# Products with v of unit 1 given to the scheduler ahead of the scores of units 2 and 3

## The chip, the cores and the metric

The kernel runs on one core of one Trainium2 chip. The metric is the device time of one execution in microseconds (us), taken as the median of several runs. Engines of the core: PE (TensorE: matmuls, with PEld for its weight loads), DVE (VectorE), ACT (ScalarE), POOL (GpSimd) and SP (SyncE, which issues all the DMAs here). Each engine runs its own instructions in a fixed order, and waits on semaphores for the others.

## The reference

Softmax attention inside chunks of 64 tokens, whose result goes through a gated feed-forward layer (sigmoid gate). All matrices are fp32.

```python
q_c, k_c, v_c = (z.reshape(8, 8, 9, 64, 64) for z in (q, k, v))       # batch, heads, chunks, 64 tokens, 64
scores = np.matmul(q_c, k_c.transpose(0, 1, 2, 4, 3)) / np.sqrt(64)
scores = scores - np.max(scores, axis=-1, keepdims=True)
attn = np.exp(scores)
attn = attn / (np.sum(attn, axis=-1, keepdims=True) + 1e-09)
x = np.matmul(attn, v_c)...reshape(4608, 512)                          # tokens x (heads x 64)
gate = 1.0 / (1.0 + np.exp(-(x @ w_gate)))                             # w_gate, w_val: 512 x 1536
out = gate * (x @ w_val) @ w_out                                       # w_out: 1536 x 512
```

## The kernel before, in words

**Tiles.** The 4608 tokens are 9 blocks `m` of 512, and the hidden width of 1536 is 12 slices `f` of 128. An fp32 number is carried as two parts, high and low (fp32r), so that each product is three matmuls: high by high, high by low, low by high. The weights come in as 64-bit words; `convert_weights(f, part)` makes the two parts of one 128x512 piece (part 0 gate, 1 value, 2 outer): on ACT L129, L130 and the cast L136 for the high part, on DVE L131, L132, L134 and L137 for the low part. Each piece is loaded by `load_weights` (L108, 512 KB per DMA) into a few raw buffers, and a buffer is loaded again only when its piece is converted.

**Attention.** It is cut into 36 units `j`; four make a block: unit 4m+2h+u gives half `h` (256 tokens) of block m, and half `u` of its 512 columns. Units 0 and 1 are the first half of block 0, units 2 and 3 its second half, units 4 to 7 block 1. A unit goes through these steps:

- `load` (L149, L152: q and k) and `load_values` (L158: v), DMAs from SP;
- `scores`: 16 PE matmuls `sc` (L170) into a PSUM tile, then on DVE the row maximum `mx` (L181). Either DVE subtracts it (L190) and the exponential comes later (capital S: units 0 and 2), or ACT does subtraction, exponential and sum in 8 activations (L195; small s: units 1 and 3);
- `softmax`: for S units the exponential on ACT (L201) and its sum on DVE (L203); for all, on DVE, L206, the reciprocal L208 and the scaling L209;
- `transposes`: 4 PE transposes `tp` (L215), evicted into `pbd` by L218 and L220 (or L222);
- `values`: 16 PE matmuls `av` (L231), evicted into the feed-forward's input `xt`: high part on ACT (L249), low part on DVE (L250).

`sc`, `tp` and `av` share two PSUM buffers (`ps_a`, tag psa): the third tile of the three kinds in a row has to wait until the first is evicted. Which tile gets which buffer follows the order in which the program calls the steps.

**Feed-forward.** `step(m, f, span)` is `hidden`: 12 matmuls `g` of the gate (L261) into bank g0, the sigmoid `hf` on ACT (L270), 12 matmuls of the value into bank g1, their product on DVE (L272), and its two parts `hh` (ACT, L274) and `hl` (DVE, L276). `down` adds its product with the outer weights into `acc` (L287). In block 0, slices 0 and 1 are done by halves: "a" is the first 256 tokens (needs units 0 and 1), "b" the rest (needs units 2 and 3). The sigmoid and the exponential need different tables on ACT; a change of table is an instruction of its own (ACT_TABLE_LOAD).

**Order.** Two strings of tokens, START and MIDDLE (L29 to L38), say in which order the program calls the steps: L, V load; S, s scores; E softmax; T, t transposes; A values; W loads and C converts weights (`C1.0`: slice 1, part 0); H is `step` (`H0.1a`: block 0, slice 1, first half); D is `down`. In START this order is no execution order: a scheduler takes the calls in that order as their priority, and sets the order of each engine from it and from its own idea of what is ready. From MIDDLE on PE keeps the order of the program (L711), and in `rest` DVE too. `rest` goes on with blocks 1 and 2, while POOL makes sums of weights (`keep_sums`, L338 to L347) which go to DRAM; blocks 3 to 8 are done in pairs by a scheme with 7 products instead of 8, with those sums as operands.

**What the change touches.** The token A1, `values(1)`: the 16 `av` matmuls of unit 1, and the ACT and DVE evictions L249 and L250 behind them.

Of the kernel before, what the change touches and what calls it, by code (L numbers as in the profile page):

```python
# [26 lines left out]


START = """  # L29
L0 L1 V0 W0o S0 s1 V1 E0 W0u t0 C0.0 E1 L2 t1 L3 C0.1 A0 W1u S2 C0.2 s3 A1 C1.0 H0.0a E2 W1o E3 C1.1  # L30
T2 W2u T3 D V3 L4 V2 C2.0 A2 C1.2 A3 L5 H0.1a H0.0b W3o D W3u C2.1 C3.0 H0.1b D s4 W4u W2o H0.2 C3.2
C2.2 W4o C3.1 C4.0 D W5u E4 C4.1 C5.0 C5.1 H0.3 D s5 C4.2 t4 E5 W6u H0.4 D W7u C6.0 V5 W6o C7.0 C6.1
H0.5 D W5o L6 C5.2 L7 C6.2 H0.6 V4 W8u C7.1 D W7o C8.0 t5 C8.1 C7.2 H0.7 D W9u
# [710 lines left out]
```

## Time and profile before

| what | us |
|---|---|
| median of 3 runs | 950.69 (950.37 to 951.47) |
| the profiled execution | 949.0 |
| its span, first to last instruction | 947.2 |
| PE busy | 927.4 (98%) |
| DVE busy | 601.1 (63%) |
| ACT busy | 340.5 (36%) |
| POOL busy | 139.0 (15%) |

Times in all rows count from the start of the span. The table says how much of the whole an engine was busy; a stage can have another bound than the whole, so the rows of the section below go by stretches of time. In a timeline an instruction's line gives its start, its length and, in brackets, how long its engine had idled before it and what ended that. Lengths overlap: in a full queue the next instruction starts before the one ahead of it has ended. The profile also gives the granted clock of PE (1.00 is 2.4 GHz, 0.50 is 1.2 GHz).

### The profile page before, as it was taken

The numbers are of one execution on the slowest core, as the hardware profiler recorded it, in microseconds if no ns is written. First come the engines' busy times: TensorE is split into PE (matmuls) and PEld (weight loads), VectorE is DVE, ScalarE is ACT, GpSimd is POOL, SyncE is SP. The second block draws the span as 40 slices with busy tenths as digits, with TensorE's granted clock in tenths as the row PEclk, the third lists the DMA queues.
The fourth block names the chain that finished last, engine by engine and source line by source line (L and its number), as shares of the span: only waits on it lengthen the run. The fifth ranks groups of instructions, "written<-read, shape, count | busy, mean of one in ns | idle before, by whom it ended". The sixth has DMA issues, their size and how long they took to land.

```text
span 947.2 us, 13080 instructions
## 1 busy us (share of the span) xinstructions
PE 927.4 (98%) x4960; PEld 762.0 (80%) x4960; DVE 601.1 (63%) x999; ACT 340.5 (36%) x556; POOL 139.0 (15%) x204
## 2 busy tenths in 40 slices
PE   6999999999999999999999999999999999999998
PEld 4778888888888887888887888888878888888886
DVE  6899973576576656766766666767686334445332
ACT  6899752233233242233142522232324221121222
POOL 1000006970079880000000000000000000000000
PEclk7999999999999999999999999999999999999999
DMA  8699894442243448657675756665565565556561
GB/s 290 210 305 298 313 305 168 134 145 78 64 137 112 134 141 312 203 200 229 205 246 207 254 186 219 211 220 201 190 222 197 193 208 183 203 184 215 218 222 45
DMA packets 81279, 189.61 MB, mean 200 GB/s; under 512 B 7488, under 2 KB 38208, under 8 KB 76608
## 3 DMA queue, kind: packets, MB, share of 16 engines
q1 hardware_dynamic: 81216, 188.77, 59.5%
q8 instruction: 39, 0.64, 0.3%
q14 instruction: 24, 0.20, 0.1%
HBM read 150.99 MB, written 37.75 MB: 199 GB/s over the span
## 4 chain that ended last, share of the span: by engine, by line
PE 81%; POOL 6%; DMA 6%; ACT 3%; DVE 2%; issue 1%; SPq 1%; POOLq 0%; ACTq 0%; DVEq 0%
PE acc L496 20%; PE cy L421 16%; PE g L261 13%; PE cz L421 11%; PE cx L421 10%; PE acc L287 6%; DMA sums<-a_both 3%; PE sc L170 3%; PE av L231 3%; POOL a_both L347 2%; POOL a_sum L344 2%; POOL a_both L346 1%; POOL a_val L338 1%; DMA out<-ob 1%; DMA wr<-sums 1%
## 5 line engine op out<-in xcount | busy, mean ns | idle before, releaser
L261 PE MATMUL g<-xt,w 128*128 128x512 f32 (+1 forms) x960 | 207.5, 371 | 3.0 <-ACT xt L249 1.3
L261 PEld LDWEIGHTS g<-xt,w 128*128 128x128 f32 x960 | 168.5, 189 | 36.3 <-ACT xt L249 1.7
L496 PE MATMUL acc<-wr,hh 128*128 128x512 f32 x576 | 177.8, 390 | 0.0
L421 PE MATMUL cy<-xc,wr 128*128 128x512 f32 x648 | 159.2, 389 | 0.9 <-DVE u L439 0.9
L421 PEld LDWEIGHTS cy<-xc,wr 128*128 128x128 f32 x648 | 121.5, 188 | 26.5 <-DVE u L439 1.3
L496 PEld LDWEIGHTS acc<-wr,hh 128*128 128x128 f32 x576 | 107.9, 188 | 22.7 <-ACT raw L242 0.3
L496 PE MATMUL acc<-wr,hl 128*128 128x512 f32 x288 | 112.7, 391 | 2.7 <-DVE hl L488 2.7
L421 PE MATMUL cz<-xc,wr 128*128 128x512 f32 x432 | 106.1, 391 | 1.1 <-DMA wr<-sums 1.1
L421 PE MATMUL cx<-xc,wr 128*128 128x512 f32 x432 | 106.0, 391 | 0.0
L560 DVE STREAM_TRANSPOSE pbd<-pr 32x256 f32<-32x256 f32 x224 | 97.6, 436 | 4.0
L488 DVE TENSOR_TENSOR hl<-hid,hh 128x512 fp32r<-128x512 f32 x72 | 49.5, 688 | 78.8 <-ACT hh L486 78.5
L421 PEld LDWEIGHTS cz<-xc,wr 128*128 128x128 f32 x432 | 80.5, 188 | 19.0 <-issue 2.5
L421 PEld LDWEIGHTS cx<-xc,wr 128*128 128x128 f32 x432 | 80.6, 188 | 17.5 <-issue 1.0
L287 PE MATMUL acc<-w,hh 128*128 128x512 f32 x288 | 90.4, 395 | 1.0 <-ACT hh L274 1.0
L486 ACT CAST hh<-hid 128x512 fp32r<-128x512 f32 x72 | 44.8, 622 | 127.1 <-PE acc L496 103.7
L338 POOL TENSOR_TENSOR a_val<-w 128x256 f32<-128x256 f32 x48 | 37.3, 798 | 202.2 <-ACT xt L249 144.7
L496 PEld LDWEIGHTS acc<-wr,hl 128*128 128x128 f32 x288 | 54.0, 188 | 16.0 <-DVE hl L488 4.8
L439 DVE TENSOR_TENSOR u<-cy,s 128x512 f32<-128x512 f32 x36 | 24.8, 688 | 63.3 <-PE cy L421 61.3
L272 DVE TENSOR_TENSOR hf<-g,hf 128x512 f32<-128x512 f32 (+1 forms) x40 | 25.4, 635 | 60.6 <-PE g L261 59.6
L287 PEld LDWEIGHTS acc<-w,hh 128*128 128x128 f32 x288 | 52.7, 188 | 13.1 <-issue 1.9
L456 DVE TENSOR_TENSOR u<-cy,s 128x512 f32<-128x512 f32 x36 | 24.9, 691 | 50.7 <-PE cy L421 50.5
L287 PE MATMUL acc<-w,hl 128*128 128x512 f32 x144 | 56.1, 389 | 0.0
(103 smaller groups left out, 1009.4 us busy)
## 6 DMA issues: line engine op xcount, KB each, us to landing
wr<-sums SPq DMA_DIRECT2D x72, 512.0 KB, 4.6
wr<-outer SPq DMA_DIRECT2D x36, 1024.0 KB, 4.9
w_raw<-w_in SPq DMA_DIRECT2D x36, 512.0 KB, 5.0
wr<-given SPq DMA_DIRECT2D x36, 512.0 KB, 3.7
sums<-a_both SPq DMA_DIRECT2D x24, 512.0 KB, 3.5
qt<-q_in SPq DMA_DIRECT2D x36, 256.0 KB, 4.4
kbd<-k_in SPq DMA_DIRECT2D x72, 128.0 KB, 4.4
vt<-v_in SPq DMA_DIRECT2D x36, 256.0 KB, 4.0
```

The source lines that it names most:

```text
L170: nc.tensor.matmul(sc[c * D:(c + 1) * D, (2 * a + t) * P:(2 * a + t + 1) * P], lhsT=s["qt"][:, a, n0:n0 + D], rhs=s["kb"][:, a, :, n0:n0 + D],
L231: nc.tensor.matmul(av[a * D:(a + 1) * D, c * P:(c + 1) * P], lhsT=s["vt"][:, a, c, :], rhs=pb[:, 4 * a + c, :, :], start=True, stop=True,)
L261: nc.tensor.matmul(ps[:, tok], lhsT=wt[f, which][:, wpart, c:c + P], rhs=x[:, part, i, tok], start=n == 0, stop=n == 11)
L272: nc.vector.tensor_tensor(out=hf, in0=pv, in1=hf, op=ALU.mult)
L287: nc.tensor.matmul(acc[m, t], lhsT=hx[:, ts], rhs=wt[f, 2][:, wpart], start=f == 0 and i == 0, stop=f == NF - 1 and i == 2,)
L338: nc.gpsimd.tensor_tensor(out=val[:, 2 * n:2 * n + 2], in0=parts[:, 0], in1=parts[:, 1], op=ALU.add)
L421: nc.tensor.matmul(bank, lhsT=lhs(wpart, c), rhs=x[:, part, c], start=start and k == 0, stop=stop and k == 5, skip_group_check=True)
L456: nc.vector.tensor_tensor(out=u3, in0=y, in1=s1, op=ALU.add)
L486: nc.scalar.copy(hh, h)
L488: nc.vector.tensor_tensor(out=hl, in0=h, in1=hh.bitcast(F32), op=ALU.subtract)
L496: nc.tensor.matmul(acc[m, t], lhsT=hx[:, ts], rhs=wo[f][:, wpart], start=f == 0 and i == 0, stop=f == NF - 1 and i == 2)
L560: nc.vector.transpose(out=pb[dst, :, c, h, i, :], in_=ps[src, h::2, k, :])
```

## The change

One token moves within START, seven places forward: A1 now stands right behind A0, ahead of the raw load of slice 1 (W1u), the scores of units 2 and 3 (S2, s3) and a conversion (C0.2).

```diff
 START = """
-L0 L1 V0 W0o S0 s1 V1 E0 W0u t0 C0.0 E1 L2 t1 L3 C0.1 A0 W1u S2 C0.2 s3 A1 C1.0 H0.0a E2 W1o E3 C1.1
+L0 L1 V0 W0o S0 s1 V1 E0 W0u t0 C0.0 E1 L2 t1 L3 C0.1 A0 A1 W1u S2 C0.2 s3 C1.0 H0.0a E2 W1o E3 C1.1
```

No instruction is added by the program, but the scheduler makes another order of all engines but POOL. ACT's order before has 36 ACT_TABLE_LOADs, and the changed one 38. In the rows below, numbers behind a name tell tiles apart (tiles may have another number in the changed program); two `sc` or `av` rows "x8" with 64 partitions stand for 16 matmuls.

**PE, first half of block 0.** `sc_228` and `sc_249` before are the scores of units 2 and 3 (`sc_240` and `sc_261` in the changed program), `av_270` (`av_225`) are the values of unit 1, g0_291 and g1_306 the first products of slice 0. Before:

```order
L231 MATMUL av_213<-pbd_89,vt_122 64x128 x8
L170 MATMUL sc_228<-kbd0_87,qt_191 64x128 x8
L261 MATMUL g0_291<-xt_222,w_178 128x256
L261 MATMUL g1_306<-xt_222,w_178 128x256
L170 MATMUL sc_249<-kbd1_88,qt_202 64x128 x8
L261 MATMUL g0_291<-xt_222,w_178 128x256 x5
L261 MATMUL g1_306<-xt_222,w_178 128x256 x3
L231 MATMUL av_270<-pbd_89,vt_159 64x128 x8
```

Changed:

```order
L231 MATMUL av_213<-pbd_89,vt_122 64x128 x8
L231 MATMUL av_225<-pbd_89,vt_159 64x128 x8
L261 MATMUL g0_291<-xt_222,w_178 128x256
L170 MATMUL sc_240<-kbd0_87,qt_191 64x128 x8
L170 MATMUL sc_261<-kbd1_88,qt_202 64x128 x8
L261 MATMUL g0_291<-xt_222,w_178 128x256 x5
L261 MATMUL g0_291<-xt_234,w_178 128x256 x6
L261 MATMUL g1_306<-xt_222,w_178 128x256 x6
L261 MATMUL g1_306<-xt_234,w_178 128x256 x6
L261 MATMUL g0_421<-xt_222,w_282 128x256
```

The values of unit 1 stand ahead of both scores, and the 24 products of slice 0 follow in one piece.

**ACT, softmax of units 2 and 3.** `early` is the tile of the exponentials, L201 that of unit 2 and L195 that of unit 3; hf_304 and hh_320 belong to slice 0 of the first half, w_282 to slice 1. Before:

```order
L201 ACTIVATE early_85<-early_85 128x512
L136 CAST w_240<-w_raw_241 128x512
L249 CAST xt_279<-av_270 128x2x256
L195 ACTIVATE early_85,sums_261<-sc_249,mx_258 128x64 x8
L270 ACT_TABLE_LOAD
L270 ACTIVATE hf_304<-g0_291 128x256
L136 CAST w_282<-w_raw_283 128x512
```

Changed:

```order
L136 CAST w_252<-w_raw_253 128x512
L129 ACTIVATE w_raw_283<-w_raw_237 128x512
L270 ACT_TABLE_LOAD
L270 ACTIVATE hf_304<-g0_291 128x256
L195 ACT_TABLE_LOAD
L195 ACTIVATE early_85,sums_273<-sc_261,mx_270 128x64 x8
L136 CAST w_282<-w_raw_283 128x512
L274 CAST hh_320<-hf_304 128x256
L201 ACTIVATE early_85<-early_85 128x512
```

Both exponentials moved behind the first sigmoid, so that the table goes to the sigmoid and back, and that of unit 2 moved behind that of unit 3.

**ACT and PE, second half of block 0.** tp_344 and tp_354 are the transposes of units 2 and 3, av_386 and av_406 their values, hf_434 the sigmoid of slice 1 for the first half. ACT before:

```order
L218 COPY pbd_89<-tp_344 64x8x64
L218 COPY pbd_89<-tp_354 64x8x64
L129 ACTIVATE w_raw_378<-w_raw_351 128x512
L130 ACTIVATE w_raw_351<-w_raw_351 128x512
L129 ACTIVATE w_raw_398<-w_raw_331 128x512
L136 CAST w_282<-w_raw_283 128x512
L249 CAST xt_222<-av_386 128x2x256
L130 ACTIVATE w_raw_331<-w_raw_331 128x512
L249 CAST xt_279<-av_406 128x2x256
```

ACT changed:

```order
L218 COPY pbd_89<-tp_344 64x8x64
L218 COPY pbd_89<-tp_354 64x8x64
L130 ACTIVATE w_raw_351<-w_raw_351 128x512
L270 ACT_TABLE_LOAD
L270 ACTIVATE hf_434<-g0_421 128x256
L136 CAST w_377<-w_raw_378 128x512
L249 CAST xt_222<-av_386 128x2x256
L249 CAST xt_234<-av_406 128x2x256
```

PE before, with g0_454 and g1_469 the products of slice 0 for the second half, and sc_555 and sc_732 the scores of units 4 and 5:

```order
L261 MATMUL g0_454<-xt_222,w_178 128x256 x6
L261 MATMUL g0_454<-xt_279,w_178 128x256
L170 MATMUL sc_555<-kbd0_87,qt_371 64x128 x7
L261 MATMUL g0_454<-xt_279,w_178 128x256 x5
L170 MATMUL sc_555<-kbd0_87,qt_371 64x128
L170 MATMUL sc_732<-kbd1_88,qt_417 64x128 x7
L261 MATMUL g1_469<-xt_222,w_178 128x256 x6
```

PE changed:

```order
L261 MATMUL g0_454<-xt_222,w_178 128x256 x6
L261 MATMUL g0_454<-xt_234,w_178 128x256
L170 MATMUL sc_555<-kbd0_87,qt_371 64x128 x5
L261 MATMUL g0_454<-xt_234,w_178 128x256 x5
L261 MATMUL g1_469<-xt_222,w_178 128x256 x6
```

The transposes' evictions and the `xt` casts now have a third table load between them, and of the scores of units 4 and 5 only 10 of 32 matmuls stand ahead of g1_469, where 30 stood before; the other 22 come in pieces of 6, 10 and 6 behind later products.

## Rows read from the trace of the kernel before

**Rows 1.** The page: busy us of each engine; granted clock of 40 slices.

```profile
PE 927.4 (98%) x4960; PEld 762.0 (80%) x4960; DVE 601.1 (63%) x999; ACT 340.5 (36%) x556; POOL 139.0 (15%) x204
PEclk7999999999999999999999999999999999999999
```

**Rows 2.** Stretches: length, busy us (instructions) by engine, granted clock, DMA share, GB/s.

```profile
17.70:42.00 24.30, 20.20 (x176) 17.04 (x175) 22.10 (x44) 21.19 (x51) 0.00 (x0) 0.93 0.64 217
42.00:56.00 14.00, 13.63 (x76) 11.60 (x75) 12.17 (x27) 10.45 (x30) 0.00 (x0) 1.00 0.90 276
56.00:74.00 18.00, 18.00 (x82) 14.55 (x82) 16.87 (x32) 17.37 (x39) 0.00 (x0) 1.00 0.91 307
265.00:947.00 682.00, 673.65 (x3439) 552.90 (x3437) 411.21 (x650) 195.06 (x271) 80.54 (x112) 1.00 0.58 196
```

**Rows 3.** Timeline of PE: start, length, what, idle time before it and releaser.

```profile
16.34 1.39 PE L170 MATMUL sc<-kbd,qt 128*64 128x128 f32 x16
...
20.39 1.98 PE L170 MATMUL sc<-kbd,qt 128*64 128x128 f32 x16
...
26.63 1.45 PE L261 MATMUL g<-xt,w 128*128 128x256 f32 x10 [0.23 <-DVE xt L250]
29.56 1.23 PE L215 MATMUL tp<-ident,early 128*128 128x128 f32 x8 [1.48 <-DVE early L209]
...
33.91 1.97 PE L231 MATMUL av<-pbd,vt 128*64 128x128 f32 x32
35.81 2.65 PE L261 MATMUL g<-xt,w 128*128 128x256 f32 x20
...
41.28 1.70 PE L261 MATMUL g<-xt,w 128*128 128x256 f32 x12
...
55.80 5.73 PE L261 MATMUL g<-xt,w 128*128 128x512 f32 x24 [0.37 <-ACT hf L270]
...
73.24 5.60 PE L261 MATMUL g<-xt,w 128*128 128x512 f32 x24
```

**Rows 4.** Stretches as in rows 2, short ones, for PE's clock.

```profile
10.00:12.00 2.00, 0.49 (x3) 0.52 (x4) 1.26 (x4) 2.00 (x16) 0.00 (x0) 0.54 1.01 410
...
22.00:23.00 1.00, 1.00 (x7) 0.70 (x4) 0.95 (x2) 1.00 (x2) 0.00 (x0) 0.50 1.00 401
...
28.00:30.00 2.00, 0.52 (x5) 0.42 (x4) 2.00 (x8) 1.97 (x5) 0.00 (x0) 1.00 0.49 139
```

**Rows 5.** Timeline of DVE.

```profile
19.29 0.69 DVE L250 TENSOR_TENSOR xt<-av,xt 128x512 fp32r<-128x512 f32 x1
...
28.72 1.29 DVE L209 TENSOR_TENSOR early<-early,inv 128x512 f32<-128x512 f32 x2
...
38.44 0.69 DVE L250 TENSOR_TENSOR xt<-av,xt 128x512 fp32r<-128x512 f32 x1
```

**Rows 6.** Timeline of ACT.

```profile
19.93 0.66 ACT L129 ACTIVATE w_raw<-w_raw 128x512 f32<-128x512 f32 x1
20.49 0.66 ACT L130 ACTIVATE w_raw<-w_raw 128x512 uint32<-128x512 uint32 x1
21.81 0.63 ACT L201 ACTIVATE early<-early 128x512 f32<-128x512 f32 x1 [0.66 <-DVE early L190]
...
25.75 0.32 ACT L195 ACTIVATE early<-sc,mx 128x64 f32<-128x64 f32 x1
...
28.25 1.28 ACT L270 ACT_TABLE_LOAD   x1
29.54 0.38 ACT L270 ACTIVATE hf<-g 128x256 f32<-128x256 f32 x1
```

**Rows 7.** Issues by line in the first 80 us: KB each, median us to landing.

```profile
w_raw<-w_in SPq DMA_DIRECT2D x24, 512.0 KB, 5.4
```

**Rows 8.** Waits after 330 us: engine line, for whom, us in total, times, longest.

```profile
PE cz L421 <- DMA wr<-sums: 1.1, 1, 1.1
```

**Rows 9.** Timeline of POOL: the start of its second run of sums.

```profile
265.13 1.94 POOL L338 TENSOR_TENSOR a_val<-w 128x256 f32<-128x256 f32 x2 [55.94 <-DMA out<-ob]
```

## Prediction

> **What bounds the kernel now.** I read the page first: PE is busy for 927.4 of the span of 947.2 us, and its clock is below full only at the very start [rows 1]. So the end moves by what PE loses or wins: idle time, and time at half clock. The stretches then show where the change can reach. From 17.7 to 42 PE is busy for 20.20 of 24.30 us, with DVE at 22.10 and ACT at 21.19; from 42 to 56 it idles 0.37 us, and from 56 to 74 not at all [rows 2]. The loss lies ahead of 42, where the softmax of units 2 and 3 has to get through ACT and DVE, both full. Behind 42, what PE has lost comes back only if it idles less later, and up to 56 there is 0.37 us to be had.
>
> **The change, part by part.** I walk through the new order with the durations of the old one.
>
> *Scores.* The `av` of unit 1 takes the place of the first `sc`, at 16.34 [rows 3]; what it reads is evicted there, since the old `sc` waited for the same buffer. The first `sc` (unit 2) now needs the buffer of unit 0's `av`, and DVE frees that at 19.29 + 0.69 = 19.98 [rows 5]. So it starts at 20.0, not 16.34, and unit 3's `sc` follows it, not ahead of 21.6. PE's clock was down to 0.54 and 0.50 after it had idled, in 10 to 12 and in 22 to 23, and the 16 `sc` matmuls then took 1.98 [rows 3, 4]. PE is as idle in 17 to 20 as before, so I take half speed here too: the two end at 23.6. Before, the second ended at 22.4. At full clock it would be about 22.2, which is the low end of this step: 1.4 sooner for PE, and 0.6 for ACT, whose casts wait for loads and DVE work too.
>
> *First products.* The other 23 `g` matmuls follow in one piece at 0.13 each (20 in 2.65 [rows 3]): done at 26.7. Before, they ended at 26.63 + 1.45 = 28.1 [rows 3]. That is the good side of the change, 1.4 us.
>
> *Softmax of units 2 and 3.* Now the bad side. DVE reduces unit 2's scores at 21.7 and only then finishes the weights that ACT casts at 23.0. With 0.56 from one ACT operation to the next (19.93 to 20.49 [rows 6]) the sigmoid's table load starts at 24.2. From there, by the rows: load 1.28, sigmoid 0.38, second load 1.28, and 2.5 for the 8 activations of unit 3 (25.75 to 28.25) [rows 6]: 29.65. Only then come the cast of slice 1's gate weights (to 30.25), `hh`, and the exponential of unit 2 (to 31.1; before, it began at 21.81 [rows 6]). PE needs that cast: it idles from 26.7 to 30.3, some 3.5 us, where its longest gap was 1.48 [rows 3]. DVE goes on with unit 2's sum at 31.2, a weight operation of the queue, two reciprocals, and the two L209 at 33.2 to 34.5. Before they ran from 28.72 to 30.01 [rows 5], so they are 4.5 us late. After its gap PE has 11 matmuls to do, `acc` and `g`, ahead of the transposes. After a gap of 1.48 the clock stayed at 1.00 [rows 4]; after one of 3.5 I expect half clock, and the 11 then last to about 34.3. That hides behind the late L209, so the clock costs little.
>
> *Second half.* The transposes run at 34.3 to 35.5, and ACT evicts them, but then reloads the sigmoid's table (36.6 to 37.9) and does a sigmoid and a weight cast ahead of the two L249 (38.7 and 39.2). DVE's second L250 ends at 41.3; before, at 38.44 + 0.69 = 39.1 [rows 5]. The last 5 matmuls of g0_454 wait for it, and g1_469 begins at 42.3, where it stood at 41.28 [rows 3]: **1.0 us**. Ahead of it stand 10 matmuls of the next scores, before 30. The other 20 have to be done later, on a PE with no idle time: at 0.062 each (32 of the same form in 1.97 [rows 3]) that is **1.2 us**.
>
> *Loads, and SP's queue.* `vt` of unit 2 no longer waits for unit 1's `av`, and the weights of slice 3 are asked for about 1.3 us sooner, since the buffer that they take is converted sooner. I count nothing for it: PE doesn't idle behind 42 for want of them.
>
> *ACT from 44 to 58.* PE would reach block 0's slice 3 at 57.5 (42.3, the 14.15 us from 41.28 to the gap ahead of 55.80, and 1.0 for 16 of the scores still owed). It needs the sigmoid of slice 2, which was 0.37 late [rows 3]. In the new order the slice 4 weights stand ahead of it, asked for at about 44.3; with 5.4 to landing [rows 7] they come at 49.7. Then 6 operations at 0.56, a load, 8 activations of unit 4, a load and the sigmoid: 58.5. If the load hides altogether, waits on DVE still make it 58.0. So PE idles 0.5 to 1.0, where it was 0.37: 0.1 to 0.7 more, **0.5** taken.
>
> *ACT from 58 to 76.* Between the sigmoids of slices 3 and 5 the new order has 23 plain ACT operations, the activations of unit 5 and two table loads: 23 x 0.56 + 2.5 + 2 x 1.28 = 17.9. PE needs 73.24 - 55.80 = 17.4 [rows 3] and 4 more matmuls: 17.7. A wait of 0.2, or 1 if a weight load is late: **0.3**. Behind that ACT has no more work left than before, while PE comes later.
>
> Sum: 1.0 + 1.2 + 0.5 + 0.3 = **3.0 us**. The lower bound is 1.9 (clock at full in the first step, and no wait at 58 and 76), the upper 4.5 (half clock until the `av` of units 2 and 3, 1 us more, and late weights). The profiled execution took 949.0, so it would take 952.0; the median lies 1.7 above that execution, and I add the 3.0 to it: **953.7**. All that follows is released by PE: even POOL's second run, at 265.13, waits for an output that PE's `acc` lets go [rows 9].
>
> On the table loads: a load and the first activation behind it follow at once, 28.25 to 29.54 [rows 6]. The Trainium skill (ScalarE: Activation LUTs, "What ACT_TABLE_LOAD costs") adds a drain to each switch and puts it at about 2.66 us. The row shows no such drain. By the skill's figure the two extra loads would cost up to 2.8 us more than I have, an estimate of 955 to 956; by the row they don't. The same page's rule for kernel authors, to do all of one table set before switching, speaks against this order, and there the rows agree.
>
> **The rivals.** I call a change of over 0.2% (1.9 us) one that a measurement can tell from none.
>
> *Not slower: the two added table loads hide.* Place: ACT, 24 to 38. The first would hide if ACT reached it while it waits for g0 (done at 25.2); the third, if it is through before the `av` of unit 2. Price: 2 x 1.28 = 2.6 off the start of g1_469, now 39.7; with the 1.2 of scores owed, and no late sigmoid at 56, that is -0.4 to -0.7, some 950.2. It decides from the point where DVE's L209 start before 31. For it: I know ACT's waits only to half a microsecond. Against it: ACT is at 21.19 of 24.30 [rows 2], and what stands ahead of each load is ready.
>
> *Given back later.* PE idles 8.35 us behind 265 [rows 2]. Where it waits for something that runs by another clock, as for the sums from DRAM (1.1 us, once [rows 8]), a later PE waits less. With the 0.37 as well that leaves +1.5: 952.2. Against it: the sums come from POOL, which starts on an output of PE's [rows 9].
>
> *Weights late.* ACT is at 17.37 of 18 us from 56 to 74, DVE at 16.87 [rows 2]. Two loads more are 2.6 us of ACT; if none of that finds a gap and the conversions fall behind PE, it comes on top: +5.6, 956.3. Against it: PE is 3 us later too, and ACT idled 3.55 of 14 us from 42 to 56 [rows 2].
>
> *Faster by over 0.2%.* The one piece of products (1.4) would have to count in full with nothing late behind it, and the softmax chain not to count at all: 948.5.
>
> **How the numbers follow.** Forecast (+1.9 to +4.5, likeliest 3.0) 0.53; weights late 0.12; given back 0.18; loads hidden 0.12; faster 0.05. Slower is 0.53 + 0.12 = 0.65, the same 0.18 + 0.12 = 0.30, faster 0.05. The range takes in the forecast, the late weights and most of what is given back: 951.6 to 956.3. It leaves out the hidden loads and the faster case, 0.17, and a little beyond.
>
> **What would show it.** PE's gap of about 3.5 us ending at 30.3, and half clock behind it; L209 at 33 to 34.5; the L249 of units 2 and 3 behind a table load, near 39; g1_469 at 42.3 and `sc` in pieces behind it; the start of PE's slice 3 at about 58, and POOL's second run at 268. It is wrong if g1_469 begins before 41, if the gap at 27 to 30 is under 2 us, or if POOL's run starts within 1 us of 265.1.

## The result, and the profile after

The changed kernel took 954.08 us (median of 12 runs, 952.16 to 957.54), the kernel before beside it 950.04: a ratio of 1.0050, with a 95% interval of 1.0034 to 1.0066, or 3.2 to 6.3 us more. So it is slower, and the time is 0.4 us from the forecast. But the sum behind the forecast was not the sum that the chip made, as the experiments show: that the two agree so closely is luck.

The first profiled execution (957.5 us) had its loads of q and k 1.7 us late, ahead of anything that the change touches. The rows here are those of a second one (956.1, run r1 below), in which the first transposes begin at 11.56; before they began at 11.51. The page, as in [rows 1]:

```profile
PE 930.5 (98%) x4960; PEld 763.8 (80%) x4960; DVE 603.0 (63%) x999; ACT 343.0 (36%) x558; POOL 135.8 (14%) x204
PEclk7999999999999999999999999999999999999999
```

The stretches, with the columns of [rows 2]:

```profile
17.70:42.00 24.30, 17.59 (x141) 15.47 (x142) 21.01 (x42) 22.18 (x50) 0.00 (x0) 0.86 0.69 237
42.00:56.00 14.00, 14.00 (x88) 11.95 (x85) 11.22 (x24) 10.31 (x20) 0.00 (x0) 1.00 0.91 288
56.00:74.00 18.00, 16.21 (x76) 12.61 (x75) 17.30 (x35) 16.37 (x41) 0.00 (x0) 0.91 0.89 294
74.00:95.00 21.00, 20.46 (x91) 16.60 (x90) 19.32 (x37) 18.92 (x44) 0.00 (x0) 1.00 0.87 275
```

PE loses in two places. Up to 42 it idles 6.71 us (4.10 before), and its mean clock is 0.86 (0.93). From 56 to 74 it idles 1.79 us at a mean clock of 0.91, where it had neither idled nor slowed down. The timeline of PE, as in [rows 3]:

```profile
20.08 3.55 PE L170 MATMUL sc<-kbd,qt 128*64 128x128 f32 x32 [0.91 <-DMA w_raw<-w_in]
23.57 3.02 PE L261 MATMUL g<-xt,w 128*128 128x256 f32 x23
30.67 0.58 PE L261 MATMUL g<-xt,w 128*128 128x256 f32 x1 [4.09 <-ACT w L136]
34.26 0.63 PE L215 MATMUL tp<-ident,early 128*128 128x128 f32 x4
40.63 0.97 PE L261 MATMUL g<-xt,w 128*128 128x256 f32 x6 [0.62 <-DVE xt L250]
42.34 2.30 PE L261 MATMUL g<-xt,w 128*128 128x256 f32 x17
57.86 0.87 PE L170 MATMUL sc<-kbd,qt 128*64 128x128 f32 x10
60.52 7.36 PE L261 MATMUL g<-xt,w 128*128 128x512 f32 x24 [1.79 <-ACT hf L270]
80.50 5.75 PE L261 MATMUL g<-xt,w 128*128 128x512 f32 x24 [0.54 <-ACT hf L270]
```

PE's clock (the third number from the end) in short stretches, as in [rows 4]:

```profile
32.00:33.00 1.00, 1.00 (x4) 0.81 (x4) 1.00 (x4) 1.00 (x3) 0.00 (x0) 0.50 0.00 0
33.00:34.00 1.00, 1.00 (x6) 0.84 (x5) 1.00 (x4) 1.00 (x3) 0.00 (x0) 0.70 0.14 29
61.00:62.00 1.00, 1.00 (x4) 0.81 (x3) 1.00 (x3) 1.00 (x3) 0.00 (x0) 0.50 1.02 406
```

The 23 products of slice 0 stand in one piece; then comes the gap of 4.09 for the cast of slice 1's weights. The second loss is the wait of 1.79 for the sigmoid of slice 2 and half clock behind it: the same 24 products took 5.73 before. The timelines of DVE, ACT, SP's queue and POOL, to be read beside [rows 5, 6, 9]:

```profile
33.42 1.29 DVE L209 TENSOR_TENSOR early<-early,inv 128x512 f32<-128x512 f32 x2
...
24.64 1.28 ACT L270 ACT_TABLE_LOAD   x1
25.93 0.39 ACT L270 ACTIVATE hf<-g 128x256 f32<-128x256 f32 x1
26.33 1.28 ACT L195 ACT_TABLE_LOAD   x1
29.96 0.66 ACT L136 CAST w<-w_raw 128x512 fp32r<-128x512 f32 x1
30.77 0.68 ACT L201 ACTIVATE early<-early 128x512 f32<-128x512 f32 x1
51.31 0.66 ACT L129 ACTIVATE w_raw<-w_raw 128x512 f32<-128x512 f32 x1 [2.27 <-DMA w_raw<-w_in]
59.87 0.60 ACT L270 ACTIVATE hf<-g 128x512 f32<-128x512 f32 x1
...
44.58 0.88 SPq L108 DMA_DIRECT2D w_raw<-w_in  x2
...
273.62 1.95 POOL L338 TENSOR_TENSOR a_val<-w 128x256 f32<-128x256 f32 x2 [57.37 <-DMA out<-ob]
```

The cast at 29.96 ends PE's gap. At 51.31 ACT takes up the first operation on slice 4's weights, for which it has waited 2.27; SP had asked for them at 44.58. The sigmoid at 59.87 is that of slice 2. In the kernel before, ACT takes those operations up behind that sigmoid, though SP asks for the same piece (the first of its three here) at much the same time:

```profile
55.15 0.60 ACT L270 ACTIVATE hf<-g 128x512 f32<-128x512 f32 x1
57.71 0.68 ACT L129 ACTIVATE w_raw<-w_raw 128x512 f32<-128x512 f32 x1
...
44.71 1.28 SPq L108 DMA_DIRECT2D w_raw<-w_in  x3
```

POOL's second run begins 8.5 late [rows 9].

### The profile page after: what moved, and what is told of

Its sections match the earlier page's. It is cut to its first block, busy times and chain, and to the rows that moved or that the text cites. A ratio compares the mean times of both kernels' runs of the same rounds, so it can differ in the third digit from the quotient of the medians.

```text
span 955.7 us, 13079 instructions
## 1 busy us (share of the span) xinstructions
PE 930.4 (97%) x4960; PEld 764.1 (80%) x4960; DVE 603.5 (63%) x999; ACT 343.5 (36%) x558; POOL 134.7 (14%) x204
## 4 chain that ended last, share of the span: by engine, by line
PE 88%; ACT 4%; DVE 4%; DMA 3%; issue 1%; SPq 0%; ACTq 0%; DVEq 0%
PE acc L496 20%; PE g L261 17%; PE cy L421 15%; PE cz L421 10%; PE cx L421 10%; PE acc L287 9%; PE sc L170 4%; PE av L231 3%; DMA w_raw<-w_in 2%; DMA kbd<-k_in 1%; ACT w_raw L129 1%; ACT w_raw L130 1%; ACT w L136 0%; DVE w L137 0%; ACT early L195 0%
```

## The experiments

All times are medians; each kernel ran on the same chip as the kernel before. A difference between two kernels that is smaller than their intervals is told as unsettled.

| run | us (runs) | before | ratio (95%) |
|---|---|---|---|
| r1 changed kernel again | 955.71 (5) | 949.90 | 1.0064 (1.0042 to 1.0085) |
| r2 loads out | 951.72 (12) | 949.90 | 1.0024 (1.0006 to 1.0041) |
| r3 softmax in old order | 955.52 (6) | 949.90 | 1.0063 (1.0043 to 1.0083) |
| r4 slice 4 late | 957.33 (5) | 949.90 | 1.0088 (1.0065 to 1.0111) |
| r5 transposes first | 954.86 (7) | 950.07 | 1.0051 (1.0028 to 1.0075) |
| r6 gap filled | 955.05 (12) | 950.07 | 1.0045 (1.0029 to 1.0062) |
| r7 loads in before | 952.46 (12) | 950.07 | 1.0022 (1.0006 to 1.0038) |
| r8 exponential called first | 950.56 (12) | 950.07 | 1.0017 (1.0003 to 1.0030) |
| r9 moved by hand | 948.64 (12) | 949.02 | 0.9993 (0.9980 to 1.0007) |
| r10 slice 4 behind sigmoid | 958.75 (6) | 949.02 | 1.0110 (1.0092 to 1.0127) |
| r11 transposes first, filled | 953.02 (7) | 949.02 | 1.0047 (1.0028 to 1.0067) |
| r12 second half as changed | 955.08 (6) | 948.87 | 1.0063 (1.0043 to 1.0084) |

To move one thing alone, most kernels have the start of each engine's order written out: lists of instructions, each tied behind the one ahead of it.

```diff
+    for order in ORDER.values():
...
+        for first, then in zip(order, order[1:]):
+            tc.add_manual_dep(made[then], first, rule, reason="order")
```

Their other edits are then given as changes of the order.

**r1, the changed kernel again.**

> The changed kernel as it is, once more, for a second profile beside kernels that differ in one thing. Theory (loss by ACT's order: table loads and late exponentials ahead of the cast of slice 1's gate weights, then the weights of slice 4 ahead of unit 4's exponentials): some 4 us over the kernel before; PE's gap of about 4 us ending near 32 and its wait of about 2 us for the sigmoid of slice 2 near 63 are there again, at the same distance from the first products. Rival 'noise of the start': the gaps are there, but the distance of POOL's second run from 265.1, which was 9.7 us, goes down by the 1.7 us that the q and k loads were late in the first profile, and by more if those waits were chance too.

Measured: 5.8 us above before, as the theory has it within the interval. Gap and wait are there again (4.09 and 1.79), and the distance of POOL's run fell from 9.7 to 8.5. The late start of the first profile was chance, gap and wait are not.

**r2, table loads out.**

```diff
-        nc.scalar.activation(hf, pg, AF.Sigmoid)
+        nc.scalar.activation(hf, pg, AF.Exp if (m, f, tok.start) == (0, 0, 0) else AF.Sigmoid)
```

> The changed kernel with each engine's order at the start written out as it stands there, and one edit: the first activation of slice 0, first half (L270) computes an exponential in place of the sigmoid, so this part of the gate is left out, and with it the two ACT_TABLE_LOADs that the change adds; all else stays where it is. Theory: ACT's chain up to the cast of slice 1's gate weights is 2.6 us shorter, PE's gap there falls from about 4 us to 1.5 to 2, g1_469 starts 2 to 2.6 us sooner, and the time falls by about 2 us against the changed kernel. Rival 'the loads hide' : ACT waits for something else, gap and time stay within 0.5 us. Rival 'the late exponential of unit 2': the gap shrinks, but the products behind it wait as much more.

Measured: 4.0 us below r1, twice what the theory gave. PE, and ACT's first operation on slice 4's weights:

```profile
28.60 0.38 PE L261 MATMUL g<-xt,w 128*128 128x256 f32 x1 [1.92 <-ACT w L136]
58.35 5.75 PE L261 MATMUL g<-xt,w 128*128 128x512 f32 x24 [1.19 <-ACT hf L270]
...
49.08 0.68 ACT L129 ACTIVATE w_raw<-w_raw 128x512 f32<-128x512 f32 x1 [1.19 <-DMA w_raw<-w_in]
```

The gap shrank as expected, from 4.09 to 1.92. What the theory had not said: the wait for the second sigmoid shrank as well, since slice 4's weights came 2.2 us sooner. "They hide" falls.

**r3, softmax in its old order.** ACT, against the changed kernel:

```diff
+L201 ACTIVATE early<-early 128x512
+L195 ACTIVATE early,sums<-sc,mx 128x64 x8
 L270 ACT_TABLE_LOAD
 L270 ACTIVATE hf<-g_291 128x256
-L195 ACT_TABLE_LOAD
-L195 ACTIVATE early,sums<-sc,mx 128x64 x8
```

> The changed kernel with its orders written out, and the softmax of units 2 and 3 put back ahead of the first sigmoid: on ACT the exponentials L201 and L195 ahead of it (so 36 table loads), on DVE the sums, reciprocals and both L209 ahead of the first product L272. PE, POOL and SP keep the changed order: products with v of unit 1 ahead of the scores, and the scores of units 4 and 5 owed. Theory: the transposes start by about 30, g1_469 within 0.5 us of its old place, and the time falls by 2.5 to 4 us against the changed kernel, to within 1.5 us of the kernel before. Rival 'PE's order' (scores later, 20 of them owed): the time stays where the changed kernel's is, within 1 us.

Measured: no change against r1 (955.52 and 955.71). My theory missed, and the rival's time came true. The timelines of DVE and PE:

```profile
27.55 1.24 DVE L209 TENSOR_TENSOR early<-early,inv 128x512 f32<-128x512 f32 x2
...
30.65 0.58 PE L261 MATMUL g<-xt,w 128*128 128x256 f32 x1 [5.44 <-ACT w L136]
34.54 1.05 PE L215 MATMUL tp<-ident,early 128*128 128x128 f32 x4
59.75 5.74 PE L261 MATMUL g<-xt,w 128*128 128x512 f32 x24 [0.61 <-ACT hf L270]
```

The softmax is done at 28.79, earlier than before (30.01 [rows 5]), and nobody uses it: PE's queue has a product of slice 1 ahead of the transposes, and that waits for the same cast until 30.65. PE's order was the next thing to bind.

**r5, transposes first as well.** PE, against r3 (the evictions L218 and L220 follow):

```diff
 L261 MATMUL g_306<-xt,w 128x256 x12
+L215 MATMUL tp<-ident,early 128x128 x8
 L261 MATMUL g_421<-xt,w 128x256
```

> The kernel r3_softmax_old_order (softmax of units 2 and 3 back ahead of the first sigmoid, 36 table loads) with one more edit: the 8 transposes of units 2 and 3 stand on PE right behind the 24 products of slice 0, ahead of the first product of slice 1 and of acc, and their evictions L218 and L220 follow them on ACT and DVE. In r3 both L209 were done at 28.8, but the transposes began at 34.5, because PE's queue had a product ahead of them that waited until 30.65 for the cast of slice 1's gate weights. Theory (ACT's order and PE's order bind one behind the other): the transposes start by 29.5, and the time falls by 1 to 2.5 us against r3. Rival 'the cast of the weights is the barrier': PE still waits till 30.6 and has the same matmuls to do behind it; only the 1 to 1.8 us of the transposes themselves move into the gap, and the later sigmoids take it back: time within 0.7 us of r3.

**r11, and the gaps filled.**

```diff
+            for _ in range(13):        # 8 ahead of the transposes, 5 behind them
+                nc.tensor.matmul(fill, lhsT=fbits, rhs=..., start=True, stop=True)
```

> The kernel r5_transposes_first with 13 extra bf16 matmuls of 512 columns that nothing uses, 8 on PE in the gap ahead of the transposes and 5 in the gap ahead of slice 1's first product. In r5 the softmax and that product were as early as in the kernel before, yet the clock was at 0.50 behind the gaps, and the time 4.8 us above. Theory (with the softmax back in its order, what is left of the first half's loss is half clock behind PE's longer gaps): transposes, acc and products run at full clock, g1_469 is 1.5 to 2.5 us sooner, and the time falls by 1 to 2 us against r5. Rival 'waits of ACT behind it take it back': PE's wait near 61 grows by as much, and the time stays within 0.5 us of r5.

Measured: r5 0.7 below r3, r11 1.8 below r5 by the medians but 4.0 above its own before, where r5 was 4.8 above: unsettled between the two. For r5 that is the rival's time. Their timelines of PE, r5 first:

```profile
29.72 1.23 PE L215 MATMUL tp<-ident,early 128*128 128x128 f32 x8 [2.20 <-DVE early L209]
61.55 5.73 PE L261 MATMUL g<-xt,w 128*128 128x512 f32 x24 [1.46 <-ACT hf L270]
```

```profile
28.34 1.23 PE L216 MATMUL tp<-ident,early 128*128 128x128 f32 x8 [1.37 <-DVE early L210]
58.71 5.73 PE L262 MATMUL g<-xt,w 128*128 128x512 f32 x24 [1.71 <-ACT hf L271]
```

(Line numbers are one higher in r6 and r11, two in r7.) In both, the transposes are as early as before [rows 3], in r11 with no half clock behind them, and PE still stops for the sigmoid of slice 2. In r11 and r2, less the late start of their first transposes against before, g1_469 begins at 41.0 and 41.4, where it stood at 41.28: with a first half about as early as before, 4.0 us (2.7 to 6.4) and 1.8 us (0.6 to 3.9) of loss are left.

**r6, the gap of the changed kernel filled** with 16 such matmuls, order otherwise as changed.

> The changed kernel with its orders written out and 16 extra bf16 matmuls of 512 columns (not used by anything) on PE in the gap ahead of slice 1's first product, so that PE is not idle there; at the 0.22 us that such a one takes at full clock they last 3.6 us and end before the gap does. Theory (the clock costs little here, since the transposes wait for the late L209): PE's clock is at full behind the gap, where the kernel without them showed 0.50 from 31 to 33, the 6 acc matmuls and 5 products take about 1.4 us less, but the time falls by 0.5 us at most. Rival 'the clock is the loss': 1.5 us or more.

Measured: 0.7 below r1, within the intervals, as the theory had it. Behind the gap the products ran at full clock, and a wait for the late L209, new here (0.88), took back what they won:

```profile
31.86 0.38 PE L262 MATMUL g<-xt,w 128*128 128x256 f32 x1 [0.56 <-ACT w L137]
35.46 0.63 PE L216 MATMUL tp<-ident,early 128*128 128x128 f32 x4 [0.88 <-DVE early L210]
62.33 7.28 PE L262 MATMUL g<-xt,w 128*128 128x512 f32 x24 [2.42 <-ACT hf L271]
...
33.00:34.00 1.00, 1.00 (x5) 0.82 (x6) 1.00 (x3) 1.00 (x3) 0.00 (x0) 1.00 0.00 0
```

Less its late start of 1.26, PE comes to the sigmoid of slice 2 at 58.65, as in r1 (58.68).

**r4 and r10, slice 4's weights behind the sigmoid of slice 2.** ACT, r10 (in r4 the four rows stand behind `hh`):

```diff
-L129 ACTIVATE w_raw<-w_raw 128x512
-L130 ACTIVATE w_raw<-w_raw 128x512
 L274 CAST hh<-hf 128x256
-L129 ACTIVATE w_raw<-w_raw 128x512
 L136 CAST w<-w_raw 128x512
-L130 ACTIVATE w_raw<-w_raw 128x512
...
 L195 ACTIVATE pr,sums<-sc,mx 128x64 x8
 L270 ACT_TABLE_LOAD
 L270 ACTIVATE hf<-g_582 128x512
+L129 ACTIVATE w_raw<-w_raw 128x512
+L130 ACTIVATE w_raw<-w_raw 128x512
+L129 ACTIVATE w_raw<-w_raw 128x512
+L130 ACTIVATE w_raw<-w_raw 128x512
```

> The changed kernel with its orders written out, and L129 and L130 of both slice 4 gate and value pieces on ACT moved behind the sigmoid and hh of slice 2, with their DVE operations behind hl. Theory: PE's wait of 2.28 us for that sigmoid falls to 0.5 or less, and the time by 1.5 to 2 us against the changed kernel. Rival 'given back': PE waits as much more at a later sigmoid (slice 3 to 5) or for the slice 4 weights, and the time stays within 0.5 us. The gap near 32 stays in both.

> The changed kernel with its orders written out, and the four operations L129, L130 of slice 4's gate and value pieces on ACT moved right behind the sigmoid of slice 2, 3 to 4 us sooner than in r4_slice4_weights_late, where they stood behind hh. In r4 PE's wait of about 2 us near 61 was gone, but a wait of 3.9 us came near 82. Theory (the weights of slice 4 ahead of unit 4's exponentials are a loss that another place avoids): no wait near 61, one of 1 us or less near 82, and 1.5 us or more below the changed kernel. Rival 'ACT has no room until 82': what is taken off the one sigmoid comes at a later one, as in r4; the time is within 1 us of the changed kernel or above it.

Measured: both slower than r1, by 1.6 (each run of r4 lies above each of r1) and, counted from its own kernel before, by 3.9. Both theories missed, and the rivals' waits came. PE and SP, r4 first, then r10:

```profile
82.64 7.07 PE L261 MATMUL g<-xt,w 128*128 128x512 f32 x24 [3.89 <-ACT hf L270]
...
56.12 10.99 SPq L108 DMA_DIRECT2D w_raw<-w_in  x5
```

```profile
81.10 8.50 PE L261 MATMUL g<-xt,w 128*128 128x512 f32 x24 [4.38 <-ACT hf L270]
...
52.55 13.05 SPq L108 DMA_DIRECT2D w_raw<-w_in  x5
```

The wait near 61 went, and a worse one came at the sigmoid of slice 4. SP shows a reason: its five next raw loads, issued within 5.32 us in r1, take 11 to 13, because a raw buffer is loaded again only when its piece is converted. In r10, DVE's part, left behind `hl`, held back ACT's casts as well (2.92 us, once). That one move can't mend the order: ACT's conversions and SP's loads are one chain.

**r7, two table loads put into the kernel before.**

```diff
+        if j == 3:
+            nc.scalar.activation(warm, warm, AF.Sigmoid)
         for i in range(8):
```

> The kernel before with its orders written out and one extra activation on ACT, a sigmoid of one column that nothing uses, right ahead of the 8 exponentials of unit 3, so that the table goes to the sigmoid's and back: two ACT_TABLE_LOADs more, nothing else. Theory (the table loads on ACT's chain are the larger part of the loss): ACT's chain is 2.7 us longer, PE's gap ahead of the transposes goes from 1.5 to about 4 us with half clock behind it, and the time rises by 2.5 to 4 us. Rival 'the loads hide': within 0.5 us of the kernel before.

Measured: 2.4 us slower, just under the range. In PE's timeline the gap ahead of the transposes grew from 1.48 [rows 3] to 4.24, and there is no wait for a sigmoid behind it, but half clock (0.50 from 33 to 39):

```profile
33.29 1.94 PE L217 MATMUL tp<-ident,early 128*128 128x128 f32 x8 [4.24 <-DVE early L211]
```

**r8, another order from the scheduler,** with unit 1's products early.

```diff
-... C0.1 A0 A1 W1u S2 C0.2 s3 C1.0 H0.0a E2 W1o E3 C1.1
+... C0.1 A0 A1 W1u S2 C0.2 s3 E2 C1.0 H0.0a W1o E3 C1.1
+        with tc.issue_after(marks["exp", 3].ins):      # the first sigmoid
```

> Products with v of unit 1 early, as in the changed kernel, but E2 (softmax of unit 2) called ahead of slice 1's conversion and slice 0, and the first sigmoid queued on ACT behind the exponentials of unit 3; the scheduler makes the orders from that, and puts the transposes of unit 2 right behind slice 0's products and L201 ahead of L195. 36 table loads. Theory: without the added loads and with the transposes ahead of slice 1's products, the early products with v cost nothing: the time is within 2 us of the kernel before, on either side. Rival 'the early products themselves cost' (both scores later, fewer scores of units 4 and 5 done by the end of slice 0): 3 us or more over the kernel before.

Measured: 0.3 to 2.9 us above before by the interval, against 4.0 to 8.1 for r1: the rival is out. The same early products, with other orders around them, lose about a quarter as much (1.0017 against 1.0064).

**r9, only the early products, by hand.** The order of the kernel before, with three rows moved (PE here; L249 and L250 likewise):

```diff
-L231 MATMUL av<-pbd,vt 64x128 x8
+L231 MATMUL av<-pbd,vt 64x128 x16
 L170 MATMUL sc<-kbd_87,qt 64x128 x8
...
-L231 MATMUL av<-pbd,vt 64x128 x8
```

> What the token's move would be alone: the orders of all engines are those of the kernel before, written out, and only the products with v of unit 1 on PE, their L249 on ACT and their L250 on DVE are moved up behind those of unit 0 (so the two scores get their PSUM buffers in the order of the changed kernel, too). Table loads, softmax, the transposes and the weights of slice 4 stand as before. Theory (the loss comes from the orders that the scheduler makes behind the move, not from the early products): within 1.5 us of the kernel before, on either side; the exponentials of unit 3 start up to 1 us sooner. Rival 'the early products themselves': the scores of unit 2 wait for a buffer until 20, all behind them is later, and the time is 3 us or more over the kernel before.

Measured: 0.9993, no difference. Its PE against [rows 3]: the scores of unit 2 stand 3.7 us later, the transposes where they were.

```profile
20.05 1.97 PE L170 MATMUL sc<-kbd,qt 128*64 128x128 f32 x16 [1.71 <-DVE xt L250]
29.57 1.23 PE L215 MATMUL tp<-ident,early 128*128 128x128 f32 x8 [1.41 <-DVE early L209]
56.27 5.76 PE L261 MATMUL g<-xt,w 128*128 128x512 f32 x24 [0.62 <-ACT hf L270]
```

The token's own move (past W1u, S2, C0.2 and s3: four places, not seven) costs nothing and brings nothing, and neither does writing the orders out.

**r12, first half by hand, second half as changed.** r9 up to the evictions of units 2 and 3; PE, ACT and DVE behind them, and SP throughout, as in the changed kernel. (SP's two orders are the same up to 35.5 us.) Against r9, the rows of PE and ACT near 50, of more that differ:

```diff
-L170 MATMUL sc<-kbd_87,qt 64x128 x7
+L170 MATMUL sc<-kbd_87,qt 64x128 x5
...
 L270 ACTIVATE hf<-g_514 128x256
 L136 CAST w<-w_raw 128x512
-L130 ACTIVATE w_raw<-w_raw 128x512
+L129 ACTIVATE w_raw<-w_raw 128x512
+L130 ACTIVATE w_raw<-w_raw 128x512
 L274 CAST hh<-hf 128x256
+L129 ACTIVATE w_raw<-w_raw 128x512
+L136 CAST w<-w_raw 128x512
+L130 ACTIVATE w_raw<-w_raw 128x512
```

> Two orders put together, written out: up to the products with v of units 2 and 3 and their evictions that of r9_moved_by_hand (which takes the time of the kernel before), and behind that on PE, ACT and DVE, and on SP throughout, the order of the changed kernel: the scores of units 4 and 5 owed, the weights of slice 4 ahead of unit 4's exponentials on ACT, SP's loads in its order. Theory (the loss is made twice, in the softmax of units 2 and 3 and once more in the queue of ACT from 44 to 58): the first half costs nothing, ACT's sigmoid of slice 2 is late by itself, PE waits 1 to 2 us for it near 57, and the time is 1.5 to 3 us over the kernel before. Rival 'one loss only' (the second wait is the first one's echo: ACT and SP are late near 58 only because all is late at 42): PE waits 0.6 us or less there, as in the kernel before, and the time is within 1 us of it.

Measured: 6.2 us above before, as much as the whole change. PE and ACT (this execution started 1.3 late: first transposes at 12.78):

```profile
30.33 1.23 PE L215 MATMUL tp<-ident,early 128*128 128x128 f32 x8 [2.09 <-DVE early L209]
61.85 7.37 PE L261 MATMUL g<-xt,w 128*128 128x512 f32 x24 [3.03 <-ACT hf L270]
...
52.65 0.66 ACT L129 ACTIVATE w_raw<-w_raw 128x512 f32<-128x512 f32 x1 [2.98 <-DMA w_raw<-w_in]
61.20 0.60 ACT L270 ACTIVATE hf<-g 128x512 f32<-128x512 f32 x1
```

Neither theory had that: the rival's echo is out (a wait of 3.03, not 0.6), but so is a loss that needs both halves. The second half's order alone makes as much as the whole change, 4.1 to 8.0 us by the interval. By the medians it is more than r2 and r11 have left, whose second half is the same: how much it costs depends on when slice 4's weights are there and on PE's clock, as the next table shows. Which of its parts costs what (ACT's order, SP's, the scores owed), r12 can't tell, for it takes them over together.

**What ties them together.** The table gives three starts (ACT's first L129 on slice 4's weights, the sigmoid of slice 2, PE's products behind it), each less the shift of that execution's first transposes against 11.51, PE's wait, and what the 24 products behind it took:

| kernel | L129 | sigmoid | PE | PE's wait | 24 products |
|---|---|---|---|---|---|
| first profile of the changed kernel | 52.72 | 61.27 | 61.93 | 2.28 | 5.74 |
| r1 | 51.26 | 59.82 | 60.47 | 1.79 | 7.36 |
| r12 | 51.38 | 59.93 | 60.58 | 3.03 | 7.37 |
| r5 | 51.37 | 59.95 | 60.60 | 1.46 | 5.73 |
| r6 | 51.87 | 60.42 | 61.07 | 2.42 | 7.28 |
| r3 | 50.19 | 58.78 | 59.43 | 0.61 | 5.74 |
| r11 | 49.15 | 57.75 | 58.40 | 1.71 | 5.73 |
| r2 | 48.98 | 57.60 | 58.25 | 1.19 | 5.75 |
| r9 | behind the sigmoid | 55.58 | 56.23 | 0.62 | 5.76 |
| before | behind the sigmoid | 55.15 | 55.80 | 0.37 | 5.73 |

In the seven kernels with the changed second half the sigmoid follows the L129 by 8.55 to 8.63 us, whatever the first half is like, and PE follows the sigmoid by 0.65. PE's slice 3 starts at 60.5 to 60.6 in r1, r5 and r12, which come to it from a bad, a mended and an undisturbed first half; but the first profile of the changed kernel has it 1.5 later than r1, so one execution places it no better than that. In these kernels a first half counts only as far as it brings slice 4's weights sooner (r2, r11). From the end of these 24 products to the end of the span, all ten executions take 884.3 to 886.7 us: what each of them loses, it has lost by there, to about 1 us.

The trace tells when these weights landed. SP asked for the first piece at 44.58 in r1, at 44.71 before and at 44.82 in r9, and it landed 6.71, 4.92 and 6.11 us later, at 51.29, 49.63 and 50.93. So the old order has it sooner by 0.4 to 1.7 us only; but there all four operations on slice 4's weights stand behind the sigmoid, and the landing holds up nothing. In r8 one of the four stands ahead (the piece landed at 49.73), and by the count of the table its sigmoid starts at 54.60 and PE's slice 3 at 55.78, without a wait. What delays the landing in the changed order is not settled. SP issues a piece of slice 11's weights ahead of slice 4's there that stood behind them before; no run moved it alone.

## Why the prediction was right, and where its working was not

- **The first half** went as forecast, nearly to the tenth. Scores 20.0 to 23.6: 20.08 to 23.63. Products done at 26.7: 26.59. The gap's end 30.3: 30.67. Cast to 30.25: 29.96 to 30.62. L209 33.2 to 34.5: 33.42 to 34.71. Transposes 34.3: 34.26. Half clock till 34.3: till some point in 33 to 34. But slice 3, forecast at about 58, started at 60.52, and POOL's second run, forecast at 268, at 273.62: what failed lies behind the first half.
- **Start of g1_469.** Forecast 42.3. The 17 products at 42.34 are 5 of g0_454 and 12 of g1_469, so it began near 43.0: 1.7 us late, not 1.0.
- **"The clock costs little"** for the gap at 30: r6 agrees (0.7, within noise).
- **The two table loads** "follow at once" and cost their 1.28: 24.64, 25.93 and 26.33 show it, and two of them in the kernel before lengthened PE's gap by 2.8 us in r7, and the time by 2.4 (0.6 to 3.6). The Trainium skill (ScalarE: Activation LUTs, "What ACT_TABLE_LOAD costs") gives 2.66 for a switch, a drain included. For two that would be 5.3, an estimate from the page's figure, and r7's gap of 2.8 more shows no such drains. (By that figure the prediction's sum would have been 953.7 + 2.8 = 956.5, not 955 to 956.) The same page's rule, to do all of one table set before switching, is borne out by r2 and r7.
- **The term of 0.5 for ACT from 44 to 58 failed.** The chain was the right one, and its length nearly so (8.8 to the sigmoid's end by my sum, 9.2 measured). But I let the weights land at 49.7, 5.4 us after the issue; they landed at 51.29. And I priced no half clock behind that wait, which cost 7.36 - 5.73 = 1.6. In r1 the term is 1.79 - 0.37 + 1.6 = 3.0; in the first profile, at full clock, it is 2.28 - 0.37 = 1.9. "Weights late" had looked for this from 56 on, by ACT's load; it came at 51, by a wait on DMA.
- **The sum failed as a sum.** 1.0 for g1_469 and 1.2 for the scores owed stood as addends ahead of 0.5. They are not: PE stops for that sigmoid anyway. Of the 22 owed, 16 run ahead of the wait (10 of them at 57.86) and only shorten it. Less the shift, PE comes to the wait at 58.68 in r1, 3.3 later than before, and at 57.56 in r12, 2.1 later; it leaves it at 60.47 and 60.58. By r12 the 6 us are there with a first half that costs nothing. Whether the changed first half costs something under the old second half, no run shows; r7 says that a first half with two more loads would, 2.4 us.
- **"SP's queue: I count nothing"** was wrong. PE's wait near 60 hangs on the landing of slice 4's weights, and r4 and r10 show SP's loads and ACT's conversions as one chain.
- **The term of 0.3 near 76** measured 0.54 (at 80.50). **Given back** happened in part: the output copies of block 1 and of block 2's start are 8.5 us later than before (258.99 and 267.53), those from 367 on 7.1; the wait of 1.1 for the sums [rows 8] is gone.

So 3.0 was near the 4.0 of the first comparison, and below the 5.8 of the second (whose interval begins at 4.0), because two terms that don't add stood in for one that was four to six times too small. The number was luck; that the change makes the kernel slower, and ACT's part in it, was not.

## What to carry to other kernels

Where a scheduler turns a list of calls into orders, a moved call is two changes: the move, and the new orders far behind it; write out the old order with the move alone (r9) before blaming either. Along a chain of barriers, delays don't add: each stage starts at the later of two arrivals, so name for every stage which one that is, and don't count what only shortens a wait. A conversion that frees a load buffer can't be moved without a look at the load queue, which stood still behind it in r4 and r10.

## What was not expected of the hardware

PE's clock behind an idle stretch doesn't follow from the length of that stretch alone. Behind a wait of 1.79 us (r1) the 24 products took 7.36 us, with a granted clock of 0.50 from 61 to 64; behind one of 2.28 (the first profile of the same kernel, same place) they took 5.74, at full clock:

```profile
63.62 5.74 PE L261 MATMUL g<-xt,w 128*128 128x512 f32 x24 [2.28 <-ACT hf L270]
...
64.00:66.00 2.00, 2.00 (x10) 1.65 (x9) 2.00 (x4) 2.00 (x5) 0.00 (x0) 1.00 1.06 361
```

That is a difference of 1.6 us between executions of one kernel, whose program has the same order in both. (The total of these two doesn't show it, since the wait ended 1.5 us later in the first profile, by the table.) Besides, the loads at the very start set the first transposes between 11.22 and 13.20 over these profiles, all ahead of any edit: two more us by chance.
